# Ordering side work behind a unit's sums, and the first batch's q in two transfers

## The chip, the cores and the metric

The kernel runs on one core of a Trainium2 chip. The metric is the device time of one execution in microseconds (us); less is better. Several executions of each kernel are timed and the median is given. One execution of the kernel before was also recorded by the hardware profiler.

## The reference: what is computed

All inputs are float32, with batch 8, sequence 576 and model width 512 (8 heads of 64):

```python
# attention without softmax, then a norm over each head
kv  = einsum('bhsd,bhse->bhde', k, v)
out = einsum('bhsd,bhde->bhse', q, kv)
x   = out / sqrt(mean(out*out, axis=-1) + 1e-6) * g_norm     # heads joined to 512 columns
# first mixer
theta = x @ w_theta
y = w_tok_r @ (x * cos(theta)) + w_tok_i @ (x * sin(theta))  # over the 576 tokens
u = x + y
x = u + relu(u @ w_ch)
# second mixer
u = x + (relu(x.T @ w_tok1) @ w_tok2).T                      # hidden 256
result = u + relu(u @ w_ch1) @ w_ch2                         # hidden 1536
```

## The kernel before

**Numbers.** Each float32 operand of a large product is split into two float16 parts, high and low, and a product is made of three matmuls (`mm3`, lines 82 to 84): high by high, high by low, low by high. A split is a ScalarE copy that rounds to the high part and a VectorE operation that subtracts it from the value. The weights come as 64-bit numbers and are decoded (`decode`, lines 120 to 130: one ScalarE copy, L123, and three VectorE operations, L128 to L130) and then split (L150, L152).

**Units.** The work is cut into units, each a Python generator. Its first part issues the matmuls; each `yield` ends a stage, and the later stages issue what other engines do with the product. For a batch they are:
- `kv` (K): the 64 by 64 products of k and v, copied to `kvbd`.
- `attend` (a0 to a4, one for each tile of 128 tokens, the last of 64): q by `kvbd`; then the square on ScalarE (L301), the sum on VectorE (L303), three GpSimd operations (L304 to L306), the multiplication (L311), high and low part (L324, L326), a transposing DMA to `xt` (L327) and the sum `R` of the parts (L330, L332). Batch 0 transposes on TensorE instead (L319).
- `rotate` (r0 to r4): theta, its evacuation (L355 on ScalarE, L356 on VectorE), three ScalarE operations for sine and cosine (L358 to L360), the multiplication by x (L362), and the parts `zh` and `zl` (L365, L367). The last, half tile is done transposed (`rotate_last`, L382 to L395) and goes through a transposing DMA (L396).
- `mix` (M00 to M13: two column chunks, 256 and 320 wide, by four row tiles): 27 matmuls each over `zh`, `zl` and the token weights; then the add to `R` (L422, VectorE), the operand `uh` (L423, ScalarE) and its low part `ul` (L426, VectorE).
- `channel` (C00 to C13): `uh`, `ul` by `w_ch`; then relu and add (L448), the operand `xs` (L449), its low parts (L456), and after each second unit a transposing DMA (L460).
- `token1` (H) and `token2` (T): the second mixer over tokens; `split_relu` (L71, L72) makes the hidden parts `hh`, `hl`, and L493 adds into `R`.

The channel products of the second mixer (`w_ch1`, `w_ch2`) follow for all batches after the mixers, from about 631 us on.

**Order.** `go(unit)` first advances every pending unit by one stage (`advance`, lines 681 to 691), then starts the new unit and appends it to the list `pending`. The order in which units are started is written out by hand (`STEADY` and `BESIDE`, lines 761 to 765): the main units of a batch, and beside them units for later batches, as r2 of the next batch beside M12, or a weight unit (`w`: `stash`, lines 186 to 221, which prepares `w_ch1` and `w_ch2`). C10 is the first channel unit that reads the sums of M10 to M13; between M13 and C10 come C02, C03, the last tile's rotation (r4) and half of K.

What the trace order gives is a priority. A planner then fixes each engine's queue: it simulates the program and lets each engine take, of what is ready by its estimates, the instruction of the highest priority. `urgent()` (line 74) raises the priority by 120 places; the sums and operands of mix, channel and token1 have it. On the chip each queue runs in the planned order. `keep_in_program_order` ties an instruction behind the one traced before it on its engine, without a wait for its end; the weights' loads and the first step of later decodes have it. All loads and transposing DMAs are issued on SP; the `stash` results go out on GpSimd's queue. There are eight PSUM banks, handed out by `bank`.

**The start.** The tiles of `w_theta` are loaded and decoded one after the other (lines 708 to 711); before the last of them `load_heads(0)` issues batch 0's k, v and q. `q` (1152 KB and a tail of 128 KB) is one tile, written by two DMAs (L257, L259). Then come kv, the five attends with the token weights (`wm`) between them, the five rotations, batch 1's kv, and the mix of batch 0 with batch 1's attends and the channel weights (`wc`) beside it (lines 769 to 771).

Of the kernel before, what the change touches and what calls it, by code (L numbers as in the profile page):

```python
# [28 lines left out]
def attn_mixer_kernel(  # L29
# [90 lines left out]
    def decode(val, raw):  # L120

        bits = val.bitcast(I32)
        first = nc.scalar.activation(val, raw[..., 1].bitcast(F32), AF.Copy, scale=2.0**-112)  # L123
        if wp:

            tc.keep_in_program_order(first)
        yield
        nc.vector.tensor_scalar(bits, bits, 3, None, ALU.logical_shift_left)  # L128
        nc.vector.scalar_tensor_tensor(bits, raw[..., 0], 29, bits, ALU.logical_shift_right, ALU.bitwise_or)
        nc.vector.scalar_tensor_tensor(bits, raw[..., 1], -(2**31), bits, ALU.bitwise_and, ALU.bitwise_or)  # L130
# [55 lines left out]
    def stash(w, name, row, cols, dst):  # L186
# [30 lines left out]
        nc.vector.scalar_tensor_tensor(lo, t[:, 1:], SW, hi, ALU.mult, ALU.subtract)  # L217
# [31 lines left out]
    def load_heads(b):  # L249
# [33 lines left out]
    def attend(o, r):  # L283
# [15 lines left out]
        x3 = x.rearrange("p (h d) -> p h d", d=D)  # L299
        yield  # L300
        nc.scalar.activation(x3, po3, AF.Square, scale=D**-0.5)  # L301
        yield
        nc.vector.tensor_reduce(ss, x3, axis=AX.X, op=ALU.add)  # L303
# [7 lines left out]
        nc.vector.tensor_tensor(x3, po3, x3, ALU.mult)  # L311
# [20 lines left out]
        nc.vector.scalar_tensor_tensor(R, xt[:, 1, :, :n], SW, R, ALU.mult, ALU.add)  # L332
# [7 lines left out]
    def rotate(o, r):  # L340
# [12 lines left out]
        f, sn = cs[:, 0], cs[:, 1]  # L353
        yield
        nc.scalar.activation(f, pt, AF.Copy, bias=MAGIC)  # L355
        nc.vector.scalar_tensor_tensor(f, f, MAGIC, pt, ALU.subtract, ALU.subtract)  # L356
        yield
        nc.scalar.activation(sn, f, AF.Sin, scale=-RAD)  # L358
        nc.scalar.activation(f, f, AF.Abs)
        nc.scalar.activation(f, f, AF.Sin, bias=hpi, scale=-RAD)  # L360
        yield
        nc.vector.tensor_tensor(cs, cs, x.unsqueeze(1).to_broadcast([P, 2, DM]), ALU.mult)  # L362
        yield
        at = slice(r, r + NR + 1, NR)
        nc.scalar.activation(zh[:, at, :], cs, AF.Copy)  # L365
        yield
        nc.vector.tensor_tensor(zl[:, at, :], cs, zh[:, at, :], ALU.subtract)  # L367

    def rotate_last(o, xt):
# [10 lines left out]
        zt = fp.tile([P, 2, DM], F16, tag="xs", name=f"zt{b}", bufs=2)  # L380
        yield
        nc.scalar.activation(f, pt, AF.Copy, bias=MAGIC)  # L382
        nc.vector.scalar_tensor_tensor(f, f, MAGIC, pt, ALU.subtract, ALU.subtract)
        yield
        nc.scalar.activation(sn[:, :, 1, :], f, AF.Sin, scale=-RAD)
        nc.scalar.activation(f, f, AF.Abs)
        nc.scalar.activation(sn[:, :, 0, :], f, AF.Sin, bias=hpi, scale=-RAD)
        R = o.R[:, :, SM:]
        for i in range(2):
            nc.vector.scalar_tensor_tensor(sn[:, :, i, :], R, 1.0 / SW, sn[:, :, i, :], ALU.mult, ALU.mult)  # L390
        yield
        sn = sn.rearrange("p k i t -> p (k i t)")
        nc.scalar.activation(zt[:, 0, :], sn, AF.Copy)
# [299 lines left out]
    def flush():  # L693
        while pending:
            advance()
# [186 lines left out]
```

## Time and profile before

| what | value |
|---|---|
| median of 3 runs | 1137.32 us (1134.44 to 1139.8) |
| the profiled execution | 1135.75 us, its span 1134.0 us |
| busy share of the span | TensorE 95%, VectorE 74%, ScalarE 50%, GpSimd 20% |
| mean granted TensorE clock | 0.98 |
| moved by DMA | 126.35 MB, mean 111 GB/s |

The span is the time from the first to the last instruction of the profiled execution; its own time has what lies around the span too. An engine's busy share counts the time in which it executes, not the time in which it waits. The granted clock is the share of full speed at which TensorE was let run. In the rows PE is TensorE's matmuls, PEld its weight loads (beside them), DVE VectorE, ACT ScalarE, POOL GpSimd and SP the queue that issues DMAs; L422 is line 422. A matmul's busy time is partly modelled, so a busy TensorE is not one at its peak.

### The profile page before, as it was taken

The page shows a single profiled execution, that of the slowest core. Times are in us where ns is not written, and L with a number is a line of the kernel's source. Part 1 is how long each engine was busy: PE and PEld are TensorE (multiplying, and loading weights), DVE is VectorE, ACT ScalarE, POOL GpSimd, SP SyncE. Part 2 cuts the span into 40 slices and gives each one's busy share as a digit, 9 for nine tenths or more (in the row PEclk, how much of TensorE's full clock was granted, in tenths as well). Part 3 has the DMA queues.
Part 4 walks back from the last instruction along what each step waited for, and adds up shares of the span by engine and source line. Part 5 has one row for each costly group of instructions (what it writes and reads, how often), then busy time and mean ns, then how long its engine had stood idle before and what let it go on. Part 6 is the DMA issues. An engine that isn't in the chain of part 4 may idle for free.

```text
span 1134.0 us, 21659 instructions
## 1 busy us (share of the span) xinstructions
PE 1078.6 (95%) x8884; PEld 817.8 (72%) x8884; DVE 839.6 (74%) x1475; ACT 563.0 (50%) x958; POOL 231.9 (20%) x290
## 2 busy tenths in 40 slices
PE   3879999999998989989999999999999999999998
PEld 3556776676875767667677777777777777777776
DVE  4998777897887887978836494867768585848584
ACT  3766536355455464653623363636354544546361
POOL 2441052462652824527100000000000000000000
PEclk9789999999999999999999999999999999999999
DMA  9535474776747647763292802011010202020101
GB/s 323 201 129 112 108 198 107 213 185 138 210 121 201 179 116 201 170 152 102 45 279 53 310 1 84 2 42 43 32 53 17 69 12 74 12 74 1 43 1 42
DMA packets 146083, 126.35 MB, mean 111 GB/s; under 512 B 93184, under 2 KB 121984, under 8 KB 145984
## 3 DMA queue, kind: packets, MB, share of 16 engines
q1 hardware_dynamic: 140608, 104.53, 33.7%
q0 software_dynamic: 5376, 20.45, 5.1%
q8 instruction: 69, 1.13, 0.4%
q14 instruction: 30, 0.25, 0.1%
HBM read 74.29 MB, written 29.88 MB: 92 GB/s over the span
## 4 chain that ended last, share of the span: by engine, by line
PE 60%; DVE 20%; DMA 8%; ACT 6%; issue 3%; POOL 1%; SPq 1%; ACTq 0%; DVEq 0%
PE na L82 4%; PE na L84 4%; PE na L83 4%; PE pa L84 4%; PE pa L83 4%; PE pa L82 4%; DMA xt<-xs 4%; DVE xs L326 2%; PE nc L82 2%; PE nc L83 2%; PE pc L84 2%; PE pc L83 2%; PE pc L82 2%; PE nc L84 2%; DVE cs L362 2%
## 5 line engine op out<-in xcount | busy, mean ns | idle before, releaser
L82 PE MATMUL py<-wmh,zh 128*128 128x256 f16 (+1 forms) x576 | 166.3, 289 | 7.4 <-ACT zh L365 3.9
L83 PE MATMUL py<-wml,zh 128*128 128x256 f16 (+1 forms) x576 | 166.0, 288 | 0.0
L84 PE MATMUL py<-wmh,zl 128*128 128x320 f16 (+1 forms) x512 | 146.5, 289 | 3.9 <-DVE zl L367 3.9
L84 PE MATMUL na<-gh,wbl 128*128 128x288 f16 x384 | 109.3, 286 | 0.0
L83 PE MATMUL pa<-o,wah 128*128 128x288 f16 x384 | 109.2, 286 | 0.0
L83 PE MATMUL na<-gl,wbh 128*128 128x288 f16 x384 | 109.1, 286 | 0.0
L82 PE MATMUL pa<-o,wah 128*128 128x288 f16 x384 | 108.4, 286 | 0.0
L84 PE MATMUL pa<-o,wal 128*128 128x288 f16 x384 | 107.8, 286 | 0.0
L82 PE MATMUL na<-gh,wbh 128*128 128x288 f16 x384 | 106.0, 286 | 0.2
L82 PE MATMUL pr<-uh,wch 128*128 128x256 f16 (+1 forms) x256 | 75.9, 297 | 8.7 <-ACT uh L423 8.7
L566 DVE TENSOR_TENSOR gl<-sum,gh 128x1152 f16<-128x1152 f32 x48 | 65.0, 1354 | 21.9 <-ACT gh L565 21.9
L83 PE MATMUL pr<-ul,wch 128*128 128x256 f16 (+1 forms) x256 | 75.9, 296 | 5.4 <-DVE ul L426 5.3
L83 PEld LDWEIGHTS <-wbh 128*128 128x128 f16 x672 | 65.7, 98 | 17.8 <-issue 0.9
L82 PEld LDWEIGHTS <-wah 128*128 128x128 f16 x672 | 65.8, 98 | 16.6
L82 PEld LDWEIGHTS <-wbh 128*128 128x128 f16 x672 | 65.7, 98 | 16.6
L84 PEld LDWEIGHTS <-wal 128*128 128x128 f16 x672 | 65.8, 98 | 16.6
L83 PEld LDWEIGHTS <-wah 128*128 128x128 f16 x672 | 65.8, 98 | 16.6
L84 PEld LDWEIGHTS <-wbl 128*128 128x128 f16 x672 | 65.7, 98 | 16.6
L84 PE MATMUL pr<-uh,wcl 128*128 128x256 f16 (+1 forms) x256 | 76.1, 297 | 0.0
L82 PEld LDWEIGHTS <-zh 128*128 128x128 f16 x576 | 57.0, 99 | 24.4 <-ACT zh L365 4.8
L305 POOL TENSOR_TENSOR ri<-ss,mhalf 128x8 f32<-128x8 f32 x40 | 72.0, 1801 | 1.4
L83 PEld LDWEIGHTS <-zh 128*128 128x128 f16 x576 | 57.0, 99 | 15.9
(292 smaller groups left out, 2917.4 us busy)
## 6 DMA issues: line engine op xcount, KB each, us to landing
q<-in_q SPq DMA_DIRECT2D x8, 1152.0 KB, 7.8
c<-u2d SPq DMA_DIRECT2D x32, 288.0 KB, 4.2
out<-c SPq DMA_DIRECT2D x64, 144.0 KB, 1.8
k<-in_k SPq DMA_DIRECT2D x24, 256.0 KB, 5.7
v<-in_v SPq DMA_DIRECT2D x24, 256.0 KB, 6.0
wa_r<-in_w_ch SPq DMA_DIRECT2D x24, 256.0 KB, 3.7
wb_r<-in_w_ch SPq DMA_DIRECT2D x24, 256.0 KB, 3.9
wad<-wa POOLq DMA_DIRECT2D x24, 224.0 KB, 2.6
```

Of the source, the lines that this page charges most:

```text
L82: nc.tensor.matmul(acc, ah, bh, start=first and i == 0, stop=False, **more)
L83: nc.tensor.matmul(acc, ah, bl, start=False, stop=False, **more)
L84: nc.tensor.matmul(acc, al, bh, start=False, stop=last and i == n - 1, **more)
L305: nc.gpsimd.tensor_tensor(ri, ss, mhalf, ALU.pow)
L326: nc.vector.tensor_tensor(xs[:, 1, :], x, xs[:, 0, :], ALU.subtract)
L362: nc.vector.tensor_tensor(cs, cs, x.unsqueeze(1).to_broadcast([P, 2, DM]), ALU.mult)
L566: nc.vector.tensor_tensor(h.lo[:, 3:], h.s, h.hi[:, 3:], ALU.subtract)
```

## The change

Four things are changed:
- `lead` notes an instruction as the latest edge of its engine; the adds, operands and low parts of mix, channel and token1 are noted. `placed` ties an instruction behind the latest edge of its engine, without a wait for the edge's end. The decode's VectorE operations, the `stash` low part, and for batch 1 and later the attend and rotate steps on ScalarE and VectorE are placed.
- Main units go to a list `leading`, which `advance` goes through before `pending`.
- For batches from 2 on, attend and rotate have additional `yield`s, so that some of their steps are traced a unit later.
- Batch 0: q's first 128 tokens are loaded ahead of the last theta tile and the remainder behind it, and the rotation's steps have raised priority.

```diff
     def split_relu(hi, lo, src):
-        nc.scalar.activation(hi, src, AF.Relu)
-        nc.vector.scalar_tensor_tensor(lo, src, 0.0, hi, ALU.max, ALU.subtract)
+        lead(nc.scalar.activation(hi, src, AF.Relu))
+        lead(nc.vector.scalar_tensor_tensor(lo, src, 0.0, hi, ALU.max, ALU.subtract))
+
+    last = {}
+
+    def lead(ins):
+
+        last[ins.ins.engine] = ins.ins
+        return ins
+
+    def placed(ins):
+
+        prev = last.get(ins.ins.engine)
+        if prev is not None:
+            tc.add_manual_dep(
+                ins.ins, prev.name,
+                mybir.DependencyInfo(mybir.DependencyClass.NoSync, mybir.DependencyReason.DATA), reason="placed",
+            )
+        return ins
...
+    def early(o):
+
+        return nullcontext() if o.b else urgent()
...
+    def beside(o):
+        return placed if o.b else lambda ins: ins
...
         qs = qT[b].rearrange("h p s -> p h s")
-        nc.sync.dma_start(o.q[:, :, :S], qs)
+        if b == 0:
+            nc.sync.dma_start(o.q[:, :, :P], qs[:, :, :P])
+        else:
+            load_q(o, 0)
+        return o
+
+    def load_q(o, at):
+        qs = qT[o.b].rearrange("h p s -> p h s")
+        nc.sync.dma_start(o.q[:, :, at:S], qs[:, :, at:])
 
         nc.sync.dma_start(o.q[:, :, S:], qs[:, :, SM:])
-        return o
...
-        nc.scalar.activation(xs[:, 0, :], x, AF.Copy)
-        yield
-        nc.vector.tensor_tensor(xs[:, 1, :], x, xs[:, 0, :], ALU.subtract)
+        if b > 1:
+            yield
+        place(nc.scalar.activation(xs[:, 0, :], x, AF.Copy))
+        yield
+        place(nc.vector.tensor_tensor(xs[:, 1, :], x, xs[:, 0, :], ALU.subtract))
         nc.sync.dma_start_transpose(xt.rearrange("p a k t -> p (a k) t"), xs.rearrange("p a d -> p (a d)"))
-        yield
-        yield
-        nc.scalar.activation(R, xt[:, 0, :, :n], AF.Copy, scale=SW)
+        for _ in range(3 if b > 1 else 2):
+            yield
+        place(nc.scalar.activation(R, xt[:, 0, :, :n], AF.Copy, scale=SW))
...
+        place = beside(o)
+        yield
+        with early(o):
+            place(nc.scalar.activation(f, pt, AF.Copy, bias=MAGIC))
+        if b > 1:
+            yield
+        with early(o):
+            place(nc.vector.scalar_tensor_tensor(f, f, MAGIC, pt, ALU.subtract, ALU.subtract))
+        yield
+        with early(o):
+            place(nc.scalar.activation(sn, f, AF.Sin, scale=-RAD))
+            nc.scalar.activation(f, f, AF.Abs)
+            nc.scalar.activation(f, f, AF.Sin, bias=hpi, scale=-RAD)
+        yield
+        with early(o):
+            place(nc.vector.tensor_tensor(cs, cs, x.unsqueeze(1).to_broadcast([P, 2, DM]), ALU.mult))
...
         with urgent():
-            nc.vector.tensor_tensor(u, py[0], u, ALU.add)
-            nc.scalar.activation(uh[:, dt, :], u, AF.Copy, scale=1.0 / SW)
+            lead(nc.vector.tensor_tensor(u, py[0], u, ALU.add))
+            lead(nc.scalar.activation(uh[:, dt, :], u, AF.Copy, scale=1.0 / SW))
...
-    pending = []
-
-    def go(unit):
+    pending, leading = [], []
+
+    def go(unit, lead=False):
         advance()
         next(unit)
-        pending.append(unit)
+        (leading if lead else pending).append(unit)
 
     def advance():
-        for g in list(pending):
-            try:
-                next(g)
-            except StopIteration:
-                pending.remove(g)
+
+        for units in (leading, pending):
+            for g in list(units):
+                try:
+                    next(g)
+                except StopIteration:
+                    units.remove(g)
...
         go(weight_tile(stg, w_theta, wt, j, DM, ST / (2.0 * math.pi), "wt"))
+    load_q(o, P)
...
-                go(UNITS[kind](o, c, i))
+                go(UNITS[kind](o, c, i), True)
```

The operations left out of this cut are wrapped in the same way: `lead` on L426, L448, L449 and L456; `placed` on L128 to L130 and L217; `place` on L301, L303, L311, L332 and on the steps of `rotate_last`, which also has two additional `yield`s for batches from 2 on (ahead of L383 and of L390).

## Rows read from the trace of the kernel before

**Rows 1.** One batch: length, busy us of PE, PEld, DVE, ACT, POOL; clock, DMA, GB/s

```profile
339.00:414.00 75.00, 70.80 (x602) 51.34 (x600) 61.91 (x103) 38.97 (x70) 35.86 (x47) 0.98 0.63 168
```

**Rows 2.** Waits of PE: line, releaser, total us, times, longest

```profile
PE pr L82 <- ACT uh L423: 8.7, 5, 2.7
...
PE pr L83 <- DVE ul L426: 5.3, 4, 1.3
...
PE py L82 <- DMA zh<-zt: 3.5, 2, 2.5
PE ph L476 <- DMA xt<-xs: 2.3, 2, 1.9
PE po L291 <- DMA q<-in_q: 1.9, 1, 1.9
```

**Rows 3.** Stretches around six stalls of PE, columns as in rows 1

```profile
205.00:213.00 8.00, 6.06 (x37) 2.87 (x34) 5.10 (x8) 3.99 (x8) 1.73 (x4) 0.79 1.00 289
266.00:274.00 8.00, 6.11 (x32) 3.54 (x31) 6.97 (x16) 5.49 (x12) 1.10 (x2) 0.79 0.69 193
339.00:348.00 9.00, 4.93 (x24) 2.80 (x22) 7.23 (x14) 5.70 (x12) 1.10 (x2) 0.81 0.46 133
414.00:423.00 9.00, 5.73 (x29) 3.28 (x29) 7.47 (x15) 5.69 (x12) 1.10 (x2) 0.81 0.49 140
490.00:495.00 5.00, 2.31 (x17) 1.51 (x16) 4.61 (x9) 3.19 (x6) 1.10 (x2) 1.00 0.38 136
564.00:571.00 7.00, 4.81 (x24) 2.69 (x23) 4.64 (x13) 2.97 (x7) 0.00 (x0) 0.76 0.43 97
```

**Rows 4.** Timeline of PE: start us, length us, instruction, idle before

```profile
333.00 0.30 PE L84 MATMUL py<-wmh,zh 128*128 128x320 f16 x1
...
339.43 0.30 PE L84 MATMUL pr<-uh,wcl 128*128 128x320 f16 x1
342.46 0.30 PE L82 MATMUL pr<-uh,wch 128*128 128x320 f16 x1 [2.73 <-ACT uh L423]
344.09 0.30 PE L83 MATMUL pr<-ul,wch 128*128 128x320 f16 x1 [1.34 <-DVE ul L426]
```

**Rows 5.** Timeline of DVE at the same stall, columns as in rows 4

```profile
336.95 0.68 DVE L356 SCALAR_TENSOR_TENSOR cs<-cs,pt 128x512 f32<-128x512 f32 x1
339.74 1.22 DVE L362 TENSOR_TENSOR cs<-cs,x 128x1024 f32<-128x1024 f32 x1 [2.12 <-ACT cs L360]
340.88 0.48 DVE L422 TENSOR_TENSOR R<-py,R 128x320 f32<-128x320 f32 x1
```

**Rows 6.** Timeline of PE, from C13 to token1 at 207 us

```profile
198.43 0.30 PE L84 MATMUL pr<-uh,wcl 128*128 128x320 f16 x1
...
207.40 0.39 PE L476 MATMUL ph<-xt,w1h 128*128 128x512 f16 x1 [1.94 <-DMA xt<-xs]
```

**Rows 7.** Timeline of DVE, the edge of C13

```profile
202.17 0.48 DVE L448 SCALAR_TENSOR_TENSOR R<-pr,R 128x320 f32<-128x320 f32 x1
```

**Rows 8.** Stretches of the start, columns as in rows 1

```profile
19.00:22.66 3.66, 2.71 (x13) 2.74 (x14) 0.01 (x1) 0.62 (x2) 0.00 (x0) 1.00 1.04 401
22.66:53.90 31.24, 22.59 (x146) 14.90 (x145) 31.17 (x46) 22.12 (x37) 16.82 (x15) 0.78 0.65 238
53.90:77.00 23.10, 15.09 (x151) 11.66 (x152) 22.36 (x33) 16.47 (x29) 8.50 (x5) 0.80 0.40 139
```

**Rows 9.** The raw tile of w_theta's last part: its issue, its landing

```profile
L116 SPq DMA_DIRECT2D wt_3r<-in_w_theta x1: 346/346/346, 12.9 to 12.9; - x1
...
DMA to landing us min/median/max: 8.7/8.7/8.7
```

**Rows 10.** The same tile's decode: one of its VectorE operations, ns

```profile
L129 DVE SCALAR_TENSOR_TENSOR wt_3v<-wt_3r,wt_3v x1: 693/693/693, 23.7 to 23.7; 128x512 int32<-128x512 int32 x1
```

**Rows 11.** Timeline of DVE, batch 1's first reduction and batch 0's first sums

```profile
67.59 0.68 DVE L303 TENSOR_REDUCE ss<-x 128x8 f32<-128x512 f32 x1
...
92.84 0.75 DVE L422 TENSOR_TENSOR R<-py,R 128x256 f32<-128x256 f32 x2
```

More of the change, by code (lines that the diff above doesn't have):

```diff
@@ L1 @@
 import math
-from contextlib import ExitStack
+from contextlib import ExitStack, nullcontext
 import numpy as np
@@ L216, in stash @@
         yield
-        nc.vector.scalar_tensor_tensor(lo, t[:, 1:], SW, hi, ALU.mult, ALU.subtract)
+        placed(nc.vector.scalar_tensor_tensor(lo, t[:, 1:], SW, hi, ALU.mult, ALU.subtract))
         yield
@@ L299, in attend @@
         x3 = x.rearrange("p (h d) -> p h d", d=D)
+        place = beside(o)
         yield
-        nc.scalar.activation(x3, po3, AF.Square, scale=D**-0.5)
+        place(nc.scalar.activation(x3, po3, AF.Square, scale=D**-0.5))
         yield
-        nc.vector.tensor_reduce(ss, x3, axis=AX.X, op=ALU.add)
+        place(nc.vector.tensor_reduce(ss, x3, axis=AX.X, op=ALU.add))
         nc.gpsimd.tensor_tensor(ss, ss, eps, ALU.add)
@@ L310, in attend @@
         yield
-        nc.vector.tensor_tensor(x3, po3, x3, ALU.mult)
+        place(nc.vector.tensor_tensor(x3, po3, x3, ALU.mult))
         n = SR if r == NR else P
@@ L380, in rotate_last @@
         zt = fp.tile([P, 2, DM], F16, tag="xs", name=f"zt{b}", bufs=2)
+        place = beside(o)
         yield
-        nc.scalar.activation(f, pt, AF.Copy, bias=MAGIC)
-        nc.vector.scalar_tensor_tensor(f, f, MAGIC, pt, ALU.subtract, ALU.subtract)
-        yield
-        nc.scalar.activation(sn[:, :, 1, :], f, AF.Sin, scale=-RAD)
-        nc.scalar.activation(f, f, AF.Abs)
-        nc.scalar.activation(sn[:, :, 0, :], f, AF.Sin, bias=hpi, scale=-RAD)
+        with early(o):
+            place(nc.scalar.activation(f, pt, AF.Copy, bias=MAGIC))
+        if b > 1:
+            yield
+        with early(o):
+            place(nc.vector.scalar_tensor_tensor(f, f, MAGIC, pt, ALU.subtract, ALU.subtract))
+        yield
+        with early(o):
+            place(nc.scalar.activation(sn[:, :, 1, :], f, AF.Sin, scale=-RAD))
+            nc.scalar.activation(f, f, AF.Abs)
+            nc.scalar.activation(sn[:, :, 0, :], f, AF.Sin, bias=hpi, scale=-RAD)
+        if b > 1:
+            yield
         R = o.R[:, :, SM:]
-        for i in range(2):
-            nc.vector.scalar_tensor_tensor(sn[:, :, i, :], R, 1.0 / SW, sn[:, :, i, :], ALU.mult, ALU.mult)
+        with early(o):
+            for i in range(2):
+                place(nc.vector.scalar_tensor_tensor(sn[:, :, i, :], R, 1.0 / SW, sn[:, :, i, :], ALU.mult, ALU.mult))
         yield
         sn = sn.rearrange("p k i t -> p (k i t)")
-        nc.scalar.activation(zt[:, 0, :], sn, AF.Copy)
+        with early(o):
+            place(nc.scalar.activation(zt[:, 0, :], sn, AF.Copy))
         yield
-        nc.vector.tensor_tensor(zt[:, 1, :], sn, zt[:, 0, :], ALU.subtract)
-        nc.sync.dma_start_transpose(
-            o.zh[:, KM - 1:, :].rearrange("p i (k d) -> p (i k) d", k=KD), zt.rearrange("p i n -> p (i n)")
+        with early(o):
+            place(nc.vector.tensor_tensor(zt[:, 1, :], sn, zt[:, 0, :], ALU.subtract))
+            nc.sync.dma_start_transpose(
+                o.zh[:, KM - 1:, :].rearrange("p i (k d) -> p (i k) d", k=KD), zt.rearrange("p i n -> p (i n)")
         )
@@ L447, in channel @@
         with urgent():
-            nc.vector.scalar_tensor_tensor(x2, pr, 0.0, x2, ALU.max, ALU.add)
-            nc.scalar.activation(xs[:, ct % 2, :n], x2, AF.Copy, scale=1.0 / SW)
+            lead(nc.vector.scalar_tensor_tensor(x2, pr, 0.0, x2, ALU.max, ALU.add))
+            lead(nc.scalar.activation(xs[:, ct % 2, :n], x2, AF.Copy, scale=1.0 / SW))
         yield
@@ L455, in channel @@
             for dst, at in lows:
-                nc.vector.scalar_tensor_tensor(xs[:, ct % 2, dst], x2[:, at], 1.0 / SW, xs[:, ct % 2, at], ALU.mult, ALU.subtract)
+                lead(nc.vector.scalar_tensor_tensor(xs[:, ct % 2, dst], x2[:, at], 1.0 / SW, xs[:, ct % 2, at], ALU.mult, ALU.subtract))
             if ct % 2:
@@ L734, in attn_mixer_kernel, with run @@
     UNITS = {"M": mix, "C": channel, "H": token1, "T": token2}
-    def run(units, o, nxt, after, beside):
+    def run(units, o, nxt, after, also):
         for u in units:
@@ L742, in run @@
             else:
-                go(UNITS[kind](o, c, i))
-            for what in beside.get(u, "").split():
+                go(UNITS[kind](o, c, i), True)
+            for what in also.get(u, "").split():
                 if what == "w":
```

25 lines of the change are left out of this document (11 added, 14 removed).

## The prediction

> **What bounds the kernel now.** I read four views in this order. The stretches by stage come first: in one batch of the steady part, 75 us long, TensorE is busy for 70.80 us, VectorE for 61.91 and ScalarE for 38.97 [rows 1]. TensorE is the engine to feed, VectorE has 13 us of room in a batch, and what can be won is TensorE's idle time and its slow clock. The list of waits comes next: whom did TensorE wait for [rows 2]? Outside the start it is mostly `uh` and `ul`, the two halves of a mix unit's sum: 8.7 and 5.3 us in nine waits. Two single waits for a transposing DMA follow. The nine waits are five stalls, one in each of five batches. I cut the trace into a stretch around each of these and around the DMA wait at 205 us, and read the granted clock [rows 3]. In five of the six the mean is 0.76 to 0.81, so TensorE ran part of the time at the lower of its two levels, 1.2 instead of 2.4 GHz, after it had stood still. The loss is (1 - clock) x length: 8 x 0.21 = 1.7 us for the stretch at 266 us, 1.7 for those at 205, 339, 414 and 564, none at 490.
>
> Last comes the order of work at one stall, the one at 339 us. The product of M13 (the last mix unit) ends at 333.30, and C10, the first channel unit that needs its sum, stands still from 339.7 to 342.46 and, after one matmul, again until 344.09 [rows 4]. The add of M13 (L422) runs on VectorE only at 340.88, 7.6 us after its product. In front of it in VectorE's queue stands the multiplication of a rotation of the next batch (L362), and that waits 2.12 us for the sines of ScalarE [rows 5]. So TensorE waits for work that nobody needs for tens of us. Of the other four stalls three have the same order, with a 2.11 us wait before L362. In the fifth, at 564, the last tile's two multiplications (L390) stand in front of the add.
>
> **Part 1, the edges.** After the change a unit's add, operand and low part are marked, and L356, L362, L367, L390, L395, the attend steps and the weights' decode are issued behind the latest marked instruction on their engine. I wrote out the order in which the stages are traced. Before, L362 of the rotation that is started beside M12 has no tie to M13's add, and the planner put it in front. After, already its L356 is tied behind M13's add and L362 behind the edge of C03. So the add can run when its product is there, at 333.3. Add, operand and low part take about 0.5 us each (L422's row: 0.48 [rows 5]), so `ul` is there near 335, and C10 asks for it at 339.4 at the earliest. The stall goes as a whole.
> - Idle time of the five: 0.6 + 1.3, 2.7 + 1.3, 1.9 + 1.3, 1.4 + 1.3 and 2.1 us: 14.0, the sum of the two `pr` lines [rows 2]. Clock: 4 x 1.7 = 6.8 [rows 3]. **Together -20.8 us** (bounds: 0, if the add is late for another reason, and -20.8).
> - The stall at 205: the product of C13 ends at 198.73 [rows 6], its edge L448 runs at 202.17 [rows 7], behind rotations again, and token1 waits 1.9 us for the transposing DMA that follows [rows 2, 6]. An edge 3 us earlier removes it: 1.9 + 1.7 of clock = 3.6. The DMA queue may still be late, so I take **-2.5** (0 to -3.6).
> - The stall at 132 (2.5 us [rows 2] and its clock): its chain ends with the DMA of batch 1's last theta tile, behind weights that wait for their loads on ScalarE. Those stay in program order, so I take **0** (-4 to +4).
>
> **What the edges cost.** They add no instruction, only order. Queued behind a tied rotation step are other rotation and attend steps and the later edges. If such a step waits for ScalarE (as L362 does, 2.12 us [rows 5]), the next edge, now one of C11 to C13, waits with it. TensorE has a unit or two of cover there. No row shows this wait, so I bound it: 0 if the extra yields keep the sines ahead, and at most one stall like the present one in each of five batches (4 us with its clock, 20 in all). I take a `ul` wait of 1.3 us [rows 4] in each: **+6.5**. VectorE has to do its 62 us in a batch of about 71 instead of 75, 87% instead of 83% [rows 1]. The rotations end some us later. They are needed in the next batch's mix, behind eight token2 units, so I cost that at nothing; if that cover were gone, mix would wait for `zl`.
>
> **Part 2, q in two transfers.** VectorE does nothing from 19.00 to 22.66 us and is busy for 31.17 of the 31.24 us behind that [rows 8]: early VectorE work is worth its length. Today 1152 KB of q lie ahead of the last theta tile, issued at 12.9 and landed 8.7 us later, near 21.6 [rows 9]. After, 256 KB do. At the 401 GB/s of that stretch [rows 8] the 1 MB moved behind it takes 2.6 us, so the tile lands near 19. Its four VectorE steps of up to 0.69 us [rows 10], 2.5 us in all, then fill the idle stretch. The first attend needs only the small transfer, so of the 1.9 us that TensorE waited for q [rows 2] a part goes; then the copy of kv's product is what is late. The remainder of q lands when the tile did before, about when the second attend ran, and one more DMA is issued on SP (0.35 us [rows 9]; nothing behind it is late). The mix weights behind both are moved by nothing.
>
> **Part 3, batch 0's rotation with priority.** It moves VectorE's work around, and adds none. TensorE is idle for 8.0 us between 53.9 and 77 and loses 4.6 to the clock (0.80) [rows 8]. But VectorE is full until then, and what rotation overtakes (decode of the mix and channel weights) must be done too. There is also a price: batch 1's attends, started beside M00 to M10, are now tied behind those units' adds. The first reduction of batch 1 runs at 67.59, the add of M00 only at 92.84 [rows 11]. In front of that add VectorE now does seven steps of batch 1's attends (0.68 each [rows 11]) and the decode of two channel tiles (eight steps of up to 0.69 [rows 10]), some 10 us in all. With rotation first, and the theta tile's 2.5 us gone, the add should come near 80; batch 1's steps then start 12 us later than now. What TensorE gains in batch 0's mix it can lose to batch 1's rotation. So gain and price meet, and I take for the whole start what the moved tile gives: **-2.5** (bounds: -12.6, all of that idle and clock, and +25, below).
>
> **Sum.** -20.8 - 2.5 + 0 + 6.5 - 2.5 = -19.3 us. The profiled execution took 1135.75 us (span 1134.0 and 1.75 around it), so 1116.5; the median of the three runs is 1.6 above it, so **1118 us**.
>
> **The rivals.**
> - *Half of it comes back.* The wait moves from M13's add to the edges of C11 to C13 or the transposing DMA behind them, because the last tile's L390 still waits for sines. For it: VectorE at 87%, and the tight 205 stall. Against: each tie is behind an edge, and the extra yields put a unit between sine and product. Price: another 10 us, **1128**.
> - *The change does not do what it says.* The planner's order stays in effect, or sums are late for a product that is late. Against: the add starts 7.6 us after its product. **1137**.
> - *Slower: the start pays.* Place: batch 1's attends behind M00's add. If that add stays at 92.84, the first reduction moves from 67.59 by 25 us [rows 11], GpSimd's serial steps follow, and TensorE runs out of work before batch 1's mix. -20.8 - 2.5 + 6.5 + 25 = +8.2: **1145**. It decides from the point where M00's add comes later than about 85 us.
> - *Slower: banks.* A rotation's product now keeps its bank of eight until the next unit's add. If all eight fill, TensorE waits about 1.3 us [rows 4] at each of 4 rotations in 6 batches: +32 with the rest: **1144**. Against: no line of the waits has TensorE waiting for a rotation's evacuation. The Trainium skill (Perfetto Trace Analysis, Optimization Strategy) reads a gap that repeats through a stretch as possibly a lack of PSUM or SBUF for the next tile. By that rule the five stalls would not go, and this rival would be the likely one; the trace puts them on data (`uh`, `ul`), not on a bank.
>
> **How the numbers follow.** Forecast 0.60, its own range 1109 to 1128; half back 0.20; no change 0.09; the start 0.07; banks 0.04. About 0.5% (5.7 us) is what a measurement of this kernel can tell from no change: faster is below 1131.6, slower above 1143. Faster: the forecast and most of the half, 0.76. Same: no change and the rest, 0.13. Slower: the two last, 0.11. The range goes from a little under the forecast's own, where the start gives too, to the no-change case: 1107 to 1138.
>
> **What would show it.** Right: M13's add within 1 us of its product; no `pr` wait for `uh` or `ul` over 1 us after 200 us; clock 1.0 around the five places; L356 and L362 behind the add; the last theta tile's steps on VectorE before 22.7; VectorE over 85% in a batch of 71 us. Wrong: new waits of `ph` for its transposing DMA or of `py` for `zl`; M00's add behind 85 us and a TensorE gap between 95 and 135; waits for a bank.

## The result, and the profile after

| what | before | after |
|---|---|---|
| median of four runs each, us | 1135.88 (1133.55 to 1139.8) | 1125.1 (1121.78 to 1126.21) |
| ratio, 95% interval | | 0.9897 [0.986, 0.9934] |
| the profiled execution, its span, us | 1135.75, 1134.0 | 1125.0, 1123.2 |
| mean granted TensorE clock | 0.98 | 0.983 |

The kernel became faster by 10.8 us, 1.0%. The forecast was 1118 us, a gain of 19.3 in the profiled execution, where 10.75 came. So the sign and the range (1107 to 1138) held, and a little over half of the gain arrived: 1125.1 lies nearer to the 1128 of the rival "half of it comes back" than to the forecast.

The list of TensorE's waits says at once that the waits of `pr` for `uh` and `ul` are gone, as forecast, and what stands in their place. First TensorE's waits, after (line, releaser, total us, times, longest), to be held against [rows 2]:

```profile
PE pt L103 <- DMA xt<-xs: 10.9, 1, 10.9
PE ph L530 <- DMA xt<-xs: 7.8, 9, 3.1
...
PE py L105 <- DVE zl L410: 1.9, 2, 1.3
...
PE py L103 <- DMA zh<-zt: 0.5, 1, 0.5
PE po L319 <- DMA q<-in_q: 0.4, 1, 0.4
```

The 14.0 us of `pr` have no line at all any more. The wait for the last theta tile's DMA (`zh<-zt`) fell from 3.5 to 0.5, and that for q from 1.9 to 0.4. New is one wait of 10.9 us of a theta product (`pt`) for a transposing DMA, and token1 (`ph`) waits nine times for its transposing DMAs, 7.8 us in all, where it waited twice for 2.3.

To see where in the kernel the time went, I cut each profiled span at two places that every kernel has: the first hidden part of batch 0's token1 (`hh`, ScalarE L71) and the first product of the second mixer's channel part (`pa`). Both starts can be read from the views by tile. After:

```profile
L71 ACT ACTIVATE hh<-ph x16: 574/597/597, 152.3 to 619.0; 128x512 f16<-128x512 f32 x16
...
L103 PE MATMUL pa<-o,wah x384: 285/286/287, 624.7 to 1094.4; 128*128 128x288 f16 x192
```

Before, `hh` began at 149.6 and `pa` at 635.4. The three parts, us, of every kernel in this study (each one profiled execution):

| kernel | start to `hh` | `hh` to `pa` | `pa` to end |
|---|---|---|---|
| before | 149.6 | 485.8 | 498.6 |
| after | 152.3 | 472.4 | 498.5 |
| edges_only | 153.5 | 471.9 | 498.6 |
| start_only | 146.2 | 486.5 | 498.5 |
| b1_free | 146.3 | 469.1 | 498.6 |
| no_yields | 151.3 | 472.1 | 498.6 |
| b1_free_zt | 146.8 | 463.1 | 498.5 |
| b1_free_one_q | 146.7 | 469.8 | 498.6 |
| b1_free_no_prio | 148.0 | 470.1 | 498.5 |
| no_lead_list | 152.4 | 471.4 | 498.5 |
| ties_only | 152.9 | 490.5 | 498.5 |
| no_ties | 149.1 | 479.6 | 498.5 |
| rotate_ties | 144.9 | 471.9 | 498.6 |
| b1_zt_old_start | 145.6 | 464.6 | 498.6 |

Up to `hh` the changed kernel loses 2.7 us (forecast: it gains 2.5). Between `hh` and `pa` it gains 13.4 (forecast: 16.8, the sum of -20.8, -2.5 and +6.5). The last part is the same. Each row is one execution, and executions of one kernel differ (before: 1131.65 to 1140.29 us in one round). As the last part hardly changes, that spread probably lies ahead of it, so a difference of a few microseconds between two rows is a hint and no more, unless the medians bear it out.

**The stall at C10.** In the batch whose stall stands in [rows 4, 5], TensorE's timeline of after shows C10 start with no wait; the product of M13 is the first line, C10's first three matmuls the others:

```profile
331.05 0.30 PE L105 MATMUL py<-wmh,zh 128*128 128x320 f16 x1
...
336.39 0.31 PE L103 MATMUL pr<-uh,wch 128*128 128x320 f16 x1
336.53 0.30 PE L104 MATMUL pr<-ul,wch 128*128 128x320 f16 x1
336.67 0.30 PE L105 MATMUL pr<-uh,wcl 128*128 128x320 f16 x1
```

VectorE's timeline in the same stretch, after:

```profile
331.25 0.48 DVE L476 TENSOR_TENSOR R<-py,R 128x320 f32<-128x320 f32 x1
...
332.07 1.47 DVE L403 TENSOR_TENSOR cs<-cs,x 128x1024 f32<-128x1024 f32 x1
333.47 0.74 DVE L480 SCALAR_TENSOR_TENSOR ul<-R,uh 128x320 f16<-128x320 f32 x1
334.13 0.48 DVE L476 TENSOR_TENSOR R<-py,R 128x320 f32<-128x320 f32 x1
334.67 1.22 DVE L410 TENSOR_TENSOR zl<-cs,zh 128x1024 f16<-128x1024 f32 x1
335.81 0.68 DVE L395 SCALAR_TENSOR_TENSOR cs<-cs,pt 128x512 f32<-128x512 f32 x1
336.41 0.48 DVE L480 SCALAR_TENSOR_TENSOR ul<-R,uh 128x320 f16<-128x320 f32 x1
```

M13's add (the second L476 shown) starts at 334.13, 2.8 us after its product ended at 331.35; before it was 7.6. In front of it stand the multiplication of an earlier rotation (L403) and M12's low part, but nothing that waits for sines. L395, the step that ran before M13's add in the kernel before, now runs behind it. The low part of M13 comes at 336.41, level with the start of C10, which asks for it a few matmuls in: the order holds with little to spare.

**Where it was given back.** Stretches of after; columns as in [rows 1]. The second is the 10.9 us gap, the third the place of the old stall at 205, the last a new one:

```profile
53.90:83.90 30.00, 26.02 (x234) 21.43 (x230) 24.35 (x40) 18.15 (x34) 1.71 (x2) 0.89 0.37 120
83.90:94.80 10.90, 0.02 (x1) 0.00 (x0) 8.59 (x15) 3.38 (x7) 10.90 (x12) 0.62 0.58 155
205.00:213.00 8.00, 7.77 (x79) 4.25 (x77) 5.34 (x12) 4.52 (x9) 1.73 (x4) 1.00 0.95 207
...
350.00:361.00 11.00, 7.94 (x50) 3.83 (x46) 3.11 (x6) 3.40 (x7) 1.73 (x4) 0.69 0.97 276
```

In the gap TensorE is busy for 0.02 us, and GpSimd, which was busy for 1.71 of the 30 us in front of it, for all of the 10.90. Four timelines of after show why. VectorE's:

```profile
78.41 0.76 DVE L476 TENSOR_TENSOR R<-py,R 128x256 f32<-128x256 f32 x2 [3.82 <-PE py L105]
...
81.35 0.68 DVE L332 TENSOR_REDUCE ss<-x 128x8 f32<-128x512 f32 x1
...
87.11 0.69 DVE L340 TENSOR_TENSOR x<-po,x 128x512 f32<-128x512 f32 x1
...
90.35 0.69 DVE L340 TENSOR_TENSOR x<-po,x 128x512 f32<-128x512 f32 x1 [0.34 <-POOL x L335]
90.95 0.68 DVE L357 TENSOR_TENSOR xs<-x,xs 128x512 f16<-128x512 f32 x1
```

GpSimd's:

```profile
82.11 0.92 POOL L333 TENSOR_TENSOR ss<-ss,eps 128x8 f32<-128x8 f32 x1 [37.96 <-DVE ss L332]
83.10 1.64 POOL L334 TENSOR_TENSOR ri<-ss,mhalf 128x8 f32<-128x8 f32 x1
84.70 1.38 POOL L333 TENSOR_TENSOR ss<-ss,eps 128x8 f32<-128x8 f32 x1
86.05 1.03 POOL L335 TENSOR_TENSOR x<-ri,gb 128x512 f32<-128x512 f32 x1
```

The transposing DMA on SP, and then the theta product on TensorE that waits for it:

```profile
91.66 1.24 SPq L358 DMA_TRANSPOSE xt<-xs  x1
```

```profile
94.81 0.61 PE L103 MATMUL pt<-wth,xt 128*128 128x512 f16 x1 [10.89 <-DMA xt<-xs]
```

M00's add came at 78.41; I had said near 80. Batch 1's first reduction (L332) waited behind it, at 81.35 instead of 67.59 [rows 11], while VectorE stood idle for 3.82 us waiting for M00's product. From there the chain to batch 1's first theta product is long, and TensorE has run out of other work at 83.9. That product needs `xt` of the first attend alone. The attend's three GpSimd steps end at 87.08 and its multiplication (the first L340) at 87.80. But its low part (L357) stands on VectorE behind the second attend's multiplication, which waits for GpSimd too, and runs only at 90.95. Its DMA is issued at 91.66, and the product starts at 94.81; before the change it started at 90.73.

The new stall in the steady part, TensorE's timeline of after at token1 of one batch:

```profile
353.79 0.61 PE L530 MATMUL ph<-xt,w1h 128*128 128x512 f16 x1 [3.06 <-DMA xt<-xs]
...
359.71 0.38 PE L534 MATMUL ph<-xt,w1rh 128*128 128x512 f16 x1
```

what VectorE did before it:

```profile
347.28 0.69 DVE L449 TENSOR_TENSOR zt<-cs,zt 128x512 f16<-128x512 f32 x1
347.88 0.55 DVE L510 SCALAR_TENSOR_TENSOR xs<-R,xs 128x256 f16<-128x256 f32 x2
```

and what SP issued:

```profile
346.23 2.46 SPq L514 DMA_TRANSPOSE xt<-xs  x1
348.78 1.25 SPq L450 DMA_TRANSPOSE zh<-zt  x1
350.14 1.36 SPq L514 DMA_TRANSPOSE xt<-xs  x1
```

The transposing DMA that token1 waits for is the third. The second, for the last theta tile of the next batch (`zh<-zt`), stands in SP's queue in front of it. C13's low parts (L510) end at 348.43, behind the theta tile's (L449), and their DMA is issued 1.7 us later, behind the tile's DMA. The matmuls behind the wait take 0.61 to 0.64 instead of 0.38 us. The granted clock of that stretch is 0.69, which by the prediction's formula costs another 11 x 0.31 = 3.4 us. That is a bound, as the stretch includes the wait itself: the fourteen steps from 353.79 to 359.71 took 5.92 us, where fourteen of the 0.21 to 0.22 at full clock take 3.0, so 2.9 us were lost.

### The profile page after: what moved, and what is told of

Read it like the earlier page. It is cut to its first block, busy times and chain, and to the rows that moved or that the text cites. A ratio compares the mean times of both kernels' runs of the same rounds, so it can differ in the third digit from the quotient of the medians.

```text
span 1123.2 us, 21650 instructions
## 1 busy us (share of the span) xinstructions
PE 1072.1 (95%) x8884; PEld 814.7 (73%) x8884; DVE 829.7 (74%) x1475; ACT 560.1 (50%) x958; POOL 229.3 (20%) x290
## 4 chain that ended last, share of the span: by engine, by line
PE 61%; DVE 18%; DMA 8%; ACT 5%; issue 4%; POOL 3%; SPq 0%; ACTq 0%; DVEq 0%; POOLq 0%
PE na L103 4%; PE na L105 4%; PE pa L104 4%; PE pa L105 4%; PE na L104 4%; PE pa L103 4%; DMA xt<-xs 4%; DVE cs L403 2%; PE py L105 2%; PE py L103 2%; PE py L104 2%; PE nc L105 2%; PE pc L104 2%; PE pc L105 2%; PE pc L103 2%
## 5 line engine op out<-in xcount | busy, mean ns | idle before, releaser
L103 PE MATMUL py<-wmh,zh 128*128 128x320 f16 (+1 forms) x576 | 165.3, 287 | 0.7 <-DMA zh<-zt 0.5
L104 PE MATMUL py<-wml,zh 128*128 128x320 f16 (+1 forms) x576 | 165.0, 287 | 0.0
L334 POOL TENSOR_TENSOR ri<-ss,mhalf 128x8 f32<-128x8 f32 x40 | 76.8, 1920 | 1.6
L103 PE MATMUL pr<-uh,wch 128*128 128x256 f16 (+1 forms) x256 | 73.1, 286 | 0.0
L105 PE MATMUL pr<-uh,wcl 128*128 128x256 f16 (+1 forms) x256 | 73.0, 286 | 0.0
L104 PE MATMUL pr<-ul,wch 128*128 128x256 f16 (+1 forms) x256 | 73.0, 286 | 0.0
L103 PEld LDWEIGHTS <-zh 128*128 128x128 f16 x576 | 56.6, 98 | 16.8 <-DMA zh<-zt 0.9
L619 ACT ACTIVATE gh<-sum 128x1152 f16<-128x1152 f32 x48 | 55.5, 1156 | 25.5 <-DVE sum L667 25.5
```

The lines of the kernel that those rows point to most:

```text
L103: nc.tensor.matmul(acc, ah, bh, start=first and i == 0, stop=False, **more)
L104: nc.tensor.matmul(acc, ah, bl, start=False, stop=False, **more)
L105: nc.tensor.matmul(acc, al, bh, start=False, stop=last and i == n - 1, **more)
L334: nc.gpsimd.tensor_tensor(ri, ss, mhalf, ALU.pow)
L619: nc.scalar.activation(h.hi[:, 3:], h.s, AF.Copy)
```

## The experiments

All ratios are against the kernel before on the same chip; its medians in the three rounds were 1135.55, 1137.48 and 1135.84 us.

### Round 1: which part does what

**edges_only**: q in one transfer again, no priority for batch 0's rotation; ties, list and yields stay.

```diff
     def early(o):
-        return nullcontext() if o.b else urgent()
+        return nullcontext()
...
-        if b == 0:
-            nc.sync.dma_start(o.q[:, :, :P], qs[:, :, :P])
-        else:
-            load_q(o, 0)
+        load_q(o, 0)
...
-    load_q(o, P)
```

> The edges, the leading list and the yields stay; q goes in one transfer and batch 0's rotation has no priority. Theory A (batch 1's attends are tied behind M00's add, and that add is late without the priority): M00's add stays near 90 us, xt of batch 1 lands 10 us later than in the changed kernel, TensorE's gap before batch 1's first theta product grows from 10.9 us to over 18, time near 1135. Theory B (the start is bound by the total of VectorE's work, whatever its order): the start ends as it did in the kernel before, time near 1123. In both the five waits of pr for uh stay away.

Measured: 1124.38 us (1122.71 to 1125.78), ratio 0.9902 [0.9884, 0.992]: that of the whole change. The gap before the theta product is there too, 10.91 us. M00's add comes early although the priority is gone:

```profile
79.15 0.76 DVE L473 TENSOR_TENSOR R<-py,R 128x256 f32<-128x256 f32 x2 [3.75 <-PE py L105]
```

So with the edges in, the start's two parts bring nothing that can be measured, and the gap is not of their making. The time is that of theory B; theory A's condition, an add near 90, did not come about.

**start_only**: only the start's parts; no tie, no list, no yields.

```diff
-        prev = last.get(ins.ins.engine)
+        prev = None
...
-        if b > 1:
-            yield
...
-        for _ in range(3 if b > 1 else 2):
+        for _ in range(2):
...
-        (leading if lead else pending).append(unit)
+        pending.append(unit)
```

> q in two transfers and batch 0's rotation with priority; no edges, no leading list, no additional yields. Theory A: M00's add comes near 80 us as in the changed kernel, and batch 1's attends are free, so the gap of 10.9 us before batch 1's first theta product is mostly gone: the first column chunk of batch 1's mix is done some 6 us earlier than the 141.6 us of before; the five waits of pr for uh are there as before (14 us and 6.8 of clock). Time near 1130. Theory B (VectorE's total binds the start): the chunk ends at 139 to 142 us, time 1133 to 1136.

Measured: 1133.05 us (1131.2 to 1138.17), ratio 0.9985 [0.9969, 1.0001], which is not told from no change. The `pr` waits are back (8.2 and 5.7 us). M00's add, with both parts of the start and no ties:

```profile
89.48 0.75 DVE L468 TENSOR_TENSOR R<-py,R 128x256 f32<-128x256 f32 x2
```

It was 92.84 before, and 79.15 with the edges alone: the ties brought it forward, not the priority. In start_only's profile `hh` comes at 146.2, 3.4 us earlier than before. Whether that is the work of the start's parts stays open, since no_ties (round 3), which has both too, gains 0.5 (149.1). Theory B for the time.

**b1_free**: the ties of attend and rotate hold only from batch 2 on.

```diff
     def beside(o):
-        return placed if o.b else lambda ins: ins
+        return placed if o.b > 1 else lambda ins: ins
```

> The changed kernel, with batch 1's attend and rotate steps no longer tied behind edges (ties from batch 2 on). Theory A (the ties of batch 1 make the 10.9 us gap): the gap falls below 3 us, and the clock stays up behind it, the first chunk of batch 1's mix ends near 134 instead of 144 us, time near 1116. Theory B (something else makes xt late, as the order of VectorE's other work): gap and time stay, 1125.

Measured: 1119.49 us (1115.77 to 1121.35), ratio 0.9856 [0.9834, 0.9878]. The gap is gone. TensorE's timeline of b1_free, the first theta product of batch 1, which stands at 94.81 in after's:

```profile
85.89 0.39 PE L103 MATMUL pt<-wth,xt 128*128 128x512 f16 x1 [0.31 <-DMA xt<-xs]
```

VectorE's timeline of b1_free, batch 1's first reduction:

```profile
64.39 0.68 DVE L332 TENSOR_REDUCE ss<-x 128x8 f32<-128x512 f32 x1
64.98 1.22 DVE L403 TENSOR_TENSOR cs<-cs,x 128x1024 f32<-128x1024 f32 x1
```

Batch 1's first reduction runs at 64.39 again, 17 us earlier, between batch 0's rotations, and `hh` comes 6.0 us earlier than after (146.3; the profiled execution is the fastest of the five, but the medians are 5.6 apart too). M00's add comes at 87.14. Theory A, with less gain than its 1116: the ties of batch 1's attends and rotations are what the start pays. Which of the two it is, rotate_ties tells below.

**no_yields**: the additional yields are taken out; ties and list stay.

```diff
-        if b > 1:
-            yield
...
-        for _ in range(3 if b > 1 else 2):
+        for _ in range(2):
```

> The changed kernel without the additional yields in attend and rotate; ties and leading list stay. Theory A (the ties alone keep the mix sums in front; the yields keep a step that waits for sines from standing in front of the next edge): no pr wait for uh over 1 us, but ph waits longer for its transposing DMA than the 7.8 us of the changed kernel, time 1127 to 1130. Theory B (the yields carry the gain): pr waits for uh come back, time 1132 or more. Theory C (the yields do nothing): 1125 and ph at 7 to 8 us.

Measured: 1125.21 us (1123.5 to 1128.58), ratio 0.9916 [0.9893, 0.9938]; no `pr` wait, `ph` waits 7.5 us in eight, and 1.5 us for VectorE's `zt` in one. The yields are not needed as long as the list is there, and the `ph` waits are not theirs. Theory C.

### Round 2: the DMA queue, and what can go

**b1_free_zt**: b1_free, and the last theta tile's two multiplications, and with them its conversion and its DMA, two more stages later.

```diff
         if b > 1:
-            yield
+            for _ in range(3):
+                yield
         R = o.R[:, :, SM:]
```

> As b1_free, and the last theta tile's multiplications, parts and transposing DMA are traced two units later (from batch 2 on), so that they stand behind C13's low part and its transposing DMA. Theory A (the waits of ph for xt come from the last tile's steps and its transposing DMA, which stand in front of C12's and C13's): the ph waits fall from 5.7 us in four to under 2, the 3.4 us of half clock behind the one at 346 us go, time 1119.5 - 5 = 1114. Theory B (C13's own edge is late on VectorE for other reasons): ph waits stay over 4 us, time 1119.

Measured: 1112.62 us (1110.17 to 1113.39), ratio 0.9788 [0.9766, 0.981]. `ph` waits for its DMA 2.4 us in five waits, none above 0.7, and the part from `hh` to `pa` is 463.1 us, 6.0 shorter than b1_free's. SP's timeline of b1_free_zt in the same batch as above: token1's transposing DMAs first, the theta tile's behind them.

```profile
338.59 3.50 SPq L515 DMA_TRANSPOSE xt<-xs  x2
342.18 1.37 SPq L451 DMA_TRANSPOSE zh<-zt  x1
```

Theory A: the order of the theta tile's steps, on VectorE and on SP, made the new waits. The edit moves both, so it does not tell their shares apart.

**b1_free_one_q** (b1_free and q in one transfer) and **b1_free_no_prio** (b1_free without the priority): the edits of edges_only, one at a time.

```diff
-        if b == 0:
-            nc.sync.dma_start(o.q[:, :, :P], qs[:, :, :P])
-        else:
-            load_q(o, 0)
+        load_q(o, 0)
...
-    load_q(o, P)
```

> As b1_free, with q in one transfer as before the change. Theory A (the theta tile's decode moves into VectorE's idle stretch near 20 us and the 2.5 us go through to the end): time 1119.5 + 2.5 = 1122, first chunk of batch 1's mix done 2.5 us later than in b1_free. Theory B (the start is bound by GpSimd's serial steps or the order behind, and the moved tile is hidden): within 1 us of 1119.5.

The other one:

```diff
-        return nullcontext() if o.b else urgent()
+        return nullcontext()
```

> As b1_free, with batch 0's rotation at its usual priority. Theory A (VectorE's work up to batch 1's mix is the same, so order brings nothing): within 1.5 us of 1119.5. Theory B (rotation first lets TensorE run ahead and the gain lasts, now that batch 1's attends are free): 1123 to 1127, the first chunk of batch 1's mix ends 4 us later or more.

Measured: 1118.47 us, 0.9843 [0.9821, 0.9864], and 1119.45 us, 0.9852 [0.9831, 0.9873]; b1_free had 0.9856. Neither part of the start brings anything that can be measured (theory B for the first, A for the second). In the profiles `hh` begins 0.4 and 1.7 us later than in b1_free, which the totals do not show.

**no_lead_list**: main units in `pending`, as before the change; ties and yields stay.

```diff
-        (leading if lead else pending).append(unit)
+        pending.append(unit)
```

> The changed kernel without the leading list: main units stay in the one pending list, the ties and yields stay. A rotation step of a unit started before the main unit is then traced before that unit's add and is tied to an earlier edge. Theory A (the list is what puts the sums in front): waits of pr for uh come back in part, time 1128 to 1133. Theory B (the additional yields already trace the rotation behind the sums): no such wait, 1125.

Measured: 1119.79 us (1118.63 to 1124.1), ratio 0.9853 [0.9831, 0.9875]; no `pr` wait, the gap at the start is there (10.1 us), `ph` waits 6.6 us in five. Theory B, and the time even lower than that of after. The profiled execution, at 1124.1 the slowest of the five, is like that of after in all three parts (152.4, 471.4, 498.5), so whether the list costs anything stays open.

### Round 3: ties, or order

**ties_only**: no list and no yields; all ties stay, and the start's two parts.

```diff
-        if b > 1:
-            yield
...
-        (leading if lead else pending).append(unit)
+        pending.append(unit)
```

> The changed kernel without the leading list and without the additional yields: only the ties are left of the edges (and the start as changed). Theory A (either list or yields are enough to put a rotation's step behind the sums; with neither, L356 of the rotation beside M12 is tied to an earlier edge and L362 to M13's add at the most): the pr waits for uh come back in part, time 1128 to 1133. Theory B (the ties carry all): no pr wait for uh over 1 us, 1122 to 1126.

Measured: 1138.66 us (1133.28 to 1143.7), ratio 1.0019 [1.0002, 1.0036]; the profiled execution was the slowest of twelve. The ties alone bring nothing. VectorE's timeline of ties_only at one C10 (the product of M13 ended at 415.0):

```profile
418.43 0.68 DVE L391 SCALAR_TENSOR_TENSOR cs<-cs,pt 128x512 f32<-128x512 f32 x1
419.03 0.48 DVE L468 TENSOR_TENSOR R<-py,R 128x320 f32<-128x320 f32 x1
421.22 1.23 DVE L399 TENSOR_TENSOR cs<-cs,x 128x1024 f32<-128x1024 f32 x1 [1.71 <-ACT cs L396]
422.36 0.49 DVE L472 SCALAR_TENSOR_TENSOR ul<-R,uh 128x320 f16<-128x320 f32 x1
```

The rotation's multiplication (L399 here) has gone behind M13's add (the L468), but it is still in front of M13's low part, and still waits 1.71 us for sines; TensorE then waits 1.01 us for `ul`. In all `pr` waits 3.1 us for `ul` in four and 2.7 for `uh` in two. The longest, 2.49 us at 345.45, is for a `uh` that came late on ScalarE: M13's add ended at 343.37, but the three sine and cosine operations (L394 to L396) stood in front of `uh` (344.95). The other waits are of `ph`, 12.6 us in six. Theory A, and worse than it said.

**no_ties**: list and yields stay, no tie.

```diff
-        prev = last.get(ins.ins.engine)
+        prev = None
```

> The changed kernel with the ties taken out; leading list, additional yields and the changed start stay. Theory A (the ties hold the planner's queue, the trace order alone is only a priority): the pr waits for uh are back, but batch 1's attends are free and the 10.9 us gap goes, time 1128 to 1133. Theory B (a rotation traced a unit later is planned later anyway): no pr waits, no gap at the start, 1117 to 1120, better than the changed kernel.

Measured: 1127.31 us (1126.03 to 1129.0), ratio 0.9918 [0.9898, 0.9938]; `pr` waits 5.7 us for `ul` in five and 1.4 for `uh` in two. It lies between the two theories, a little below the time of theory A. VectorE's timeline of no_ties at the stall of [rows 5]:

```profile
338.91 1.22 DVE L403 TENSOR_TENSOR cs<-cs,x 128x1024 f32<-128x1024 f32 x1 [2.11 <-ACT cs L400]
340.06 0.48 DVE L476 TENSOR_TENSOR R<-py,R 128x320 f32<-128x320 f32 x1
```

The old order stands here, with the same wait for sines. List and yields alone shorten the part from `hh` to `pa` by 6.2 us, and with ties by 13.4. The ties are needed for the five stalls to go as a whole, and need the list or the yields beside them.

**rotate_ties**: only rotations are tied; attend, decode and `stash` are free.

```diff
-        place = beside(o)
+        place = lambda ins: ins
...
-        placed(nc.vector.scalar_tensor_tensor(lo, t[:, 1:], SW, hi, ALU.mult, ALU.subtract))
+        nc.vector.scalar_tensor_tensor(lo, t[:, 1:], SW, hi, ALU.mult, ALU.subtract)
```

(The three operations of the decode are freed in the same way; the `place` above is that of attend.)

> The changed kernel with the ties on the rotation's steps alone; attend steps and the weights' decode are free. Theory A (the rotation's steps were what stood in front of the sums, and the attends' ties make the 10.9 us gap): no pr waits for uh, gap under 3 us, 1117 to 1120. Theory B (the attend and decode steps step in where the rotation's were): pr waits of 1 us or more come back, 1123 or more.

Measured: 1118.93 us (1117.13 to 1119.91), ratio 0.9843 [0.9821, 0.9865]; no `pr` wait, no gap at the start, `hh` at 144.9, `ph` waits 6.7 us in seven. Theory A: with list and yields, the ties on the rotations are enough to take the stalls away, and batch 1's among them do no harm. What this run and b1_free both set free is batch 1's attends alone, so their ties make the gap. What the ties on the decode and `stash` do by themselves was not run.

**b1_zt_old_start**: b1_free_zt with the old start (one transfer of q, no priority), so the edits shown above together.

> As b1_free_zt, with q in one transfer and batch 0's rotation without priority, so that of the change only the order of the steady part is left. Theory A (the start's two parts bring nothing, alone or together): within 2 us of b1_free_zt's 1112.6, the ratio to the kernel before within 0.002 of 0.979. Theory B (together they bring what each alone did not show): 1116 or more, ratio 0.982 or more.

Measured: 1110.58 us (1109.5 to 1113.31), ratio 0.9776 [0.9756, 0.9797]. Theory A: it does without both parts of the start, and is the fastest run here, 2.2% below before. The rotation ties alone with the later theta tile were not run together.

## Why the prediction was right or wrong

**The five C10 stalls: -20.8, right.** All `pr` waits are gone, and the granted clock, 0.76 to 0.81 around four of them [rows 3], is 1.00 from 100 us to 620 us but for the new stall shown above. The stretches of after, columns as in [rows 1]:

```profile
100.00:350.00 250.00, 245.84 (x2148) 178.20 (x2148) 208.01 (x384) 136.94 (x257) 92.66 (x117) 1.00 0.62 157
361.00:620.00 259.00, 256.19 (x2125) 188.64 (x2125) 202.07 (x354) 126.92 (x226) 99.54 (x127) 1.00 0.57 150
```

With the new waits taken away (b1_free_zt) the part from `hh` to `pa` is 22.7 us shorter than before, against the 23.3 of the first two terms. What failed is the detail "M13's add within 1 us of its product": it is 2.8, and that was early enough. My reason was short, too: I gave it to the ties, and ties_only shows that the tie by itself moves the wait from the add to the low part behind it. A tie keeps a step behind the latest edge that is traced before it; only a step that is traced late enough is behind the edge that counts.

**The stall at 205: -2.5.** The wait there is 0.23 us where it was 1.94, and the clock 1.00 where it was 0.79 [rows 3]: 1.7 + 1.7 = -3.4, close to the bound of -3.6.

**The stall at 132: 0.** It went, but into the gap at the start. In the five kernels with a gap of 10 or 11 us near 90 us (after, edges_only, no_yields, no_lead_list, ties_only) TensorE's timeline has no such wait; in the other nine, before among them, which have no gap, it stands between 129 and 136 us, 1.0 to 3.0 us long. So the change did not remove it: it was covered.

**The new waits: +6.5, undersized.** From `hh` to `pa`: -20.8 - 3.4 + x = -13.4, so x = 10.8 us. Its parts are the `ph` waits beyond those of before (7.8 - 0.23 at 205, less 0.4 that stood before, 7.2) and the clock behind the longest one (2.9; 3.4 by the prediction's formula). The remaining 0.7 is not accounted for. The mechanism is that of the rival "half of it comes back", whose price was another 10 us: the wait moved to the transposing DMA behind the edges of C11 to C13, through the last tile's steps. Its reason was another, though: at the stall at 353.79 the tile's multiplications (L442, the L390 of before, at 344.87 and 346.08) start without a wait for sines. I had not looked for the order in which that tile's low part and DMA come first: 0.69 us on VectorE, and 1.25 us of issue on SP in front of the DMA that is waited for. In b1_free_zt, with both behind, no wait of `ph` for its DMA is above 0.7 us.

**The start: -2.5, measured +2.7 at `hh`, the covered wait at 132 included. This is the step that failed:** "So gain and price meet". The theta tile did what I said. Its landing and its steps after (tile view, the last line from issue to landing):

```profile
L150 DVE SCALAR_TENSOR_TENSOR wt_3v<-wt_3r,wt_3v x1: 691/691/691, 20.6 to 20.6; 128x512 int32<-128x512 int32 x1
L151 DVE SCALAR_TENSOR_TENSOR wt_3v<-wt_3r,wt_3v x1: 693/693/693, 21.3 to 21.3; 128x512 int32<-128x512 int32 x1
...
DMA to landing us min/median/max: 6.8/6.8/6.8
```

It landed at 19.3 (19 was said), and VectorE's 0.01 busy us between 19 and 22.66 [rows 8] are 2.67 now; the last of the four steps starts at 22.8.

But no gain came of it that can be measured: edges_only has the time of the whole change, and start_only's ratio includes 1. Nor can the 3.4 us of start_only's profile be put down to the start's parts, as no_ties, with both, comes to `hh` at 149.1, and b1_zt_old_start, with neither, at 145.6. That M00's add came at 78.41, near the 80 I had said, was partly luck: I had counted on the rotation's priority and the theta tile too, but edges_only has the add at 79.15 without these, and start_only at 89.48 with them. What brings it forward are the ties, which take batch 1's attends from in front of it.

And the price was there: 6.0 us, the difference in `hh` between after and b1_free. The rival "the start pays" had the place right and the condition wrong. It decides, I wrote, if the add is later than 85. In the five kernels with the gap the add comes at 78.2 to 79.5, in the nine without it at 85.7 to 92.8. What decides is that the attends are tied behind it at all. The first reduction came 14 us later (I had said 12), and from it to the theta product there are another 13.5 us, longer than TensorE had work. The rival's price was far too high, 25 us where 6.0 came, as TensorE had work for a part of that delay, and as b1_free, without the gap, has waits of its own ahead of `hh` (1.36 us at 131 us, and 2.6 us for `w1rh`).

**VectorE.** I said over 85% in a batch of 71 us. In two stretches of 71 us without the new stall, from 266 and from 420 us, it was busy for 58.80 and 60.82 us, 83 and 86%. VectorE did not become the bound.

**Banks and no change.** No product of a rotation waits for a bank in the list; the one wait that may be for a bank is in batch 0's attends, 0.84 us of `px` at 48.41 for the operation that reads the `px` before. (The rival's 1144 leaves the +6.5 of the sum out; with it, it is about 1150.) The Trainium skill (Perfetto Trace Analysis, Optimization Strategy) says that a repeating gap can mean that SBUF or PSUM is short for the next tile. Here it had another cause: the five gaps went with the same eight banks, by order alone. "No change" is out by the interval, [0.986, 0.9934].

## What to carry to other kernels

When the engine that bounds the kernel waits for a short operation on a free engine, look at what stands ahead of that operation in the free engine's queue, and whether that waits itself; moving it behind was worth the whole stall and its slow clock here. A tie must name the edge that counts, and must be put only on the work that was in the way: here the rotations, while the same tie on batch 1's attends starved the next stage. A number that comes true proves no reason: M00's add came near 80 without the step that was to bring it there. And follow the moved work to its own queues: the moved tile's DMA was in front of another that TensorE needed next.

## What the runs showed of the hardware

- One wait of 3.06 us cost more than itself: the stretch around it had a granted clock of 0.69, and its matmuls, 0.61 to 0.64 us instead of 0.38, lost 2.9 us more. A wait of 1.33 us in another batch (at 280.53) had a clock of 1.00 from 276 to 282 us. But the length of the wait alone does not decide. Single waits of 2.85, 2.91 and 3.20 us (b1_free at 346.20, rotate_ties at 348.08, ties_only at 439.68) are likewise followed by matmuls of 0.61 to 0.64 us, and so are shorter ones of 1.99 and 2.13 us (no_yields at 211.16, no_lead_list at 355.18, 0.63). Behind 2.55, 2.73 and 2.81 us (b1_free_no_prio at 350.35, edges_only at 356.07, b1_free_one_q at 347.41) the matmuls take 0.38. These runs do not show what makes the difference.
- The part from `pa` to the end took 498.5 or 498.6 us in all fourteen profiled executions, whatever lay before it. The differences between these profiles are all in the mixers.
- Early VectorE work was not worth its length: with the same edges, `hh` came at 146.8 with the start's two parts and at 145.6 without (b1_free_zt and b1_zt_old_start), though VectorE was busy for 2.89 us between 19 and 22.66 us with them and for 0.07 without. The medians, 1112.62 and 1110.58, show no gain either.
